# Weight halves 64 bytes past a multiple of 256, and tokens that begin at column 0, 12 or 16

## The chip, the cores and the metric

One core of a Trainium2 chip runs the kernel. The metric is the device time of one execution in microseconds. TensorE (PE in the profile) multiplies; VectorE (DVE), ScalarE (ACT) and GpSimd (POOL) work elementwise; SyncE (SP) issues most transfers. SBUF is the on-chip memory of 128 partitions, PSUM the one that TensorE writes. An address below is a byte offset within a partition of SBUF, the same in all partitions.

## The reference

Attention with a decay in place of the softmax, then a mixture of experts in two levels with one expert for each token. There are N = 4608 tokens of 512 values, and 16 experts (4 groups of 4), each with a first layer of 512 x 1024 and a second of 1024 x 512, in float32.

```python
ret = scale * (q @ k.T) * Dmat[None]          # gamma ** (i - j) for i >= j, else 0
x = (ret @ v).transpose(0, 2, 1, 3).reshape(4608, 512)
g_idx = argmax(x @ w_group); g_w = softmax at g_idx
e_idx = argmax(xg @ w_expert[g]); e_w = softmax at e_idx
h = maximum(xg[mask_e] @ w1[g, e], 0.0)
out[tok_idx] = (g_w * e_w)[:, None] * (h @ w2[g, e])
```

## The kernel before

Some 36 tiles of 128 tokens go through the attention first; each token's expert is found, and its row of x, already scaled by the product of the two weights, is scattered to its expert's region in HBM (`xs`). The expert stage follows, in 17 passes. Pass 0 takes the first 256 tokens of an expert that was picked early, while the attention still runs; passes 1 to 15 take the other experts in falling order of their counts; pass 16 takes the rest of pass 0's expert.

A pass of an expert (1 to 15) has its tokens in the columns. `xturn` turns them by VectorE into `xTf`, with 512 features as 4 chunks (`kc`) of 128 partitions. `xsplit` splits them into a rounded half `xTh` (ScalarE) and the rest `xTl` (VectorE), both of type float32r, in buffers of 4 x 384 columns. The weights come by DMA in pieces (`r`) and `wsplit` splits them in the same way into `wh0`, `wl0` (first layer) and `wh1`, `wl1` (second layer), each half 4096 bytes in a partition, three buffers for each name. `layer1` makes for each of 8 blocks of 128 hidden values (`f`) the products wh x xh, wh x xl and wl x xh over 4 chunks, 12 matmuls into one bank of PSUM. ScalarE's Relu writes `hh`, VectorE the difference `hl`, 384 columns each. `layer2` makes 12 products from them in the same manner, into 4 banks. So an expert pass has 8 x 24 = 192 matmuls. In all of them the weights are stationary (128 x 128) and the tokens move, as many columns as the pass is wide.

The width of a pass is chosen on the chip. `by_width` compares the expert's count with `LOWS[p]` and branches to matmuls that are `LOWS[p]` wide, or to those that are `CAPS[p]` wide (`CS[p]`). In pass 1 the first four blocks of layer one are always 356 wide. All writes of ScalarE and VectorE are `CS[p]` wide in either case.

Passes 0 and 16 differ: in pass 0 the first six blocks multiply plain float32 (`whole`), and in its second layer, and in both layers of pass 16, the tokens are stationary and the weights move.

The order of work is the order of the program, pinned on each engine; in a pass, block f's first layer stands before block f-1's second layer, so that at the seam of two passes one block of the new width stands before the last block of the old. Allocation goes pool by pool, in the order of the tiles in the program. In the built kernel, `wh`, `wl`, `xTh`, `xTl`, `hh` and `hl` all begin at a multiple of 256 bytes; the unused tile `lead` of 32 bytes is there ahead of them.

Of the kernel before, what the change touches and what calls it, by code (L numbers as in the profile page):

```python
# [7 lines left out]
F32 = mybir.dt.float32  # L8
F32R = mybir.dt.float32r
# [3 lines left out]
ALU = mybir.AluOpType  # L13
AX = mybir.AxisListType

P = 128
# [6 lines left out]
NKC = DM // P  # L23
NFC = F // P
CAPS = [384, 356, 342, 330, 322, 314, 310, 304, 298, 292, 288, 284, 280, 274, 266, 256]
LOWS = [0, 332, 318, 316, 316, 298, 298, 298, 292, 290, 278, 278, 268, 260, 252, 238]
CMAX = CAPS[0]
EARLY = 256
PICK = 26
WHOLE = 6  # L30
# [13 lines left out]
WQ = DQ + 4  # L44
NB = CMAX // 32
LINE = 64
# [21 lines left out]
def moe_retention(ctx, tc, qk, kv, wgt, w1, w2, c_f, out):  # L68
# [5 lines left out]
    wp = ctx.enter_context(tc.tile_pool(name="wp", bufs=1))  # L74
# [52 lines left out]
    dve, act, pool, sp = [Ordered(e_) for e_ in (nc.vector, nc.scalar, nc.gpsimd, nc.sync)]  # L127
# [29 lines left out]
    wsp = {}  # L157
    CS = [EARLY] + CAPS[1:] + [CAPS[0] - EARLY]
    NPASS = E + 1
# [10 lines left out]
    def whole(p, f):  # L170

        return p == 0 and f < WHOLE
# [6 lines left out]
    xTs = {}  # L179
# [7 lines left out]
    def ring(name):  # L187

        return gp.tile([P, NRING], F32, name=name, tag="ring", bufs=4)[:, 0 : NB * WQ]

    def nblocks(p):
        return -(-CS[p] // 32)
# [4 lines left out]
    def xpair(nm):  # L197
        return [
            gp.tile([P, NKC, CMAX], F32R, name=f"xT{x_}_{nm}", tag="xT" + x_, bufs=2) for x_ in "hl"
        ]  # L200
# [11 lines left out]
    def by_width(p, part):  # L212

        if p not in wide:
            part(CS[p])
            return
        with tc.If(wide[p] <= LOWS[p]) as narrow:
            part(LOWS[p])
        with narrow.Else():
            part(CS[p])  # L220

    def expert_of(p):
        ereg[p] = nc.values_load(
            order[0:1, p : p + 1] if p % E > 1 else eai[p % E][0:1, 0:1],
            engines=[mybir.EngineType.SP], min_val=0, max_val=E - 1,
        )

    def xload(p):
# [3 lines left out]
        if p not in ereg:  # L232
            expert_of(p)
        r0 = EARLY if p == E else 0
        nb = nblocks(p)
# [20 lines left out]
    def xpad(p):  # L256

        apart("xs", pool.indirect_dma_start(
            out=xs, out_offset=bass.IndirectOffsetOnAxis(ap={0: pad0, 1: pad1}.get(p, pads[:, p % E : p % E + 1]), axis=0),
            in_=zero, in_offset=None, bounds_check=E * NS - 1, oob_is_err=False,  # L260
        ))

    def pad(rows, e, n, cap):

        pd = sm.tile([P, 2], F32, name=f"pd_{rows.name}", tag="pd")
        dve.tensor_scalar(pd[:, 0:1], sln[:, 0:1], n, None, ALU.add)
        dve.tensor_scalar(pd[:, 1:2], pd[:, 0:1], float(cap), float(E * NS), ALU.is_ge, ALU.mult)
        dve.tensor_tensor(pd[:, 0:1], pd[:, 0:1], pd[:, 1:2], ALU.add)
        dve.scalar_tensor_tensor(rows, e, float(NS), pd[:, 0:1], ALU.mult, ALU.add)
# [4 lines left out]
    def xturn(p, part, of):  # L274

        if part == 0:
            xTs[p] = xpair(f"m{p}")
            if p == 0:

                xTf[p] = wp.tile([P, NKC, EARLY], F32, name="xTf_0", tag="wl1", bufs=3)  # L280
            else:
                xTf[p] = ring(f"xTf_{p}")[:, 0 : NKC * CMAX].rearrange("p (k c) -> p k c", k=NKC)
        nb = nblocks(p)
# [4 lines left out]
        )  # L288

    def xsplit(p, kc):  # L290
        hi, lo = xTs[p]
        C = CS[p]
        x_ = xTf[p][:, kc, :C]
        act.copy(hi[:, kc, :C], x_)
        dve.tensor_tensor(lo[:, kc, :C], x_, hi[:, kc, :C].bitcast(F32), ALU.subtract)

    def ids(p):

# [17 lines left out]
    for bp in range(B // 2):  # L316
        for j in range(9):
            if j < 8:
                b, c = 2 * bp + j // 4, j % 4
# [26 lines left out]

    sm = ctx.enter_context(tc.tile_pool(name="sm", bufs=2))
    gp = ctx.enter_context(tc.tile_pool(name="gp", bufs=1))
    ps_tr = ctx.enter_context(tc.tile_pool(name="ps_tr", bufs=1, space=PSUM))
    ps_st = ctx.enter_context(tc.tile_pool(name="ps_st", bufs=1, space=PSUM))  # L350
    ps_sm = ctx.enter_context(tc.tile_pool(name="ps_sm", bufs=2, space=PSUM))
# [189 lines left out]
    def taken():  # L541
# [5 lines left out]
        dve.tensor_reduce(c0, k2, AX.X, ALU.add)  # L547
        pad(pad0, f0, c0, EARLY)
        xpad(0)
# [13 lines left out]
    def layer1(p, f):  # L563
        i = p * NPIECE + f // 2
        C = CS[p]
        if (p, f) in ((0, 0), (0, 1)):
            ph = ps_st.tile([P, CMAX], F32, name=f"ph_{p}_{f}", tag="tr")
        elif p == 0:
            ph = psy.tile([P, CMAX], F32, name=f"ph_{p}_{f}", tag=f"py{f % 2}")
        else:  # L570
            if f % 4 not in phs:
                pool_ = (ps_sm, ps_tr, ps_sm, ps_st)[f % 4]
                phs[f % 4] = pool_.tile([P, DM], F32, name=f"ph_{f % 4}", tag="sm" if f % 2 == 0 else "tr")
            ph = phs[f % 4]
        cs = slice((f % 2) * P, (f % 2) * P + P)
        if (p, f) == (0, 0):

            hh = wp.tile([P, NKC, EARLY], F32, name="hh_0_0", tag="wl0", bufs=3)[:, 0]
        else:
            hh = mp.tile([P, CMAX], F32R, name=f"hh_{p}_{f}", tag="hh", bufs=4)  # L580
        if whole(p, f):
            for kc in range(NKC):
                pe.matmul(  # L583
                    ph[:, :C], raws[i][0][:, kc, cs], xTf[p][:, kc, :C], start=kc == 0, stop=kc == NKC - 1
                )
            hf = hh if f == 0 else hh.bitcast(F32)
            act.activation(hf[:, :C], ph[:, :C], AF.Relu)
            hts[p, f] = (hf, None)
            return
        wh, wl = wsp[i, 0]  # L590
        xh, xl = xTs[p]

        def sums(w):
            n = 0
            for kc in range(NKC):
                for a, b in ((wh, xh), (wh, xl), (wl, xh)):
                    pe.matmul(  # L597
                        ph[:, :w], a[:, kc, cs], b[:, kc, :w], start=n == 0, stop=n == 3 * NKC - 1
                    )
                    n += 1  # L600

        if (p, f) in ((1, 0), (1, 1), (1, 2), (1, 3)):
            sums(C)
        else:
            by_width(p, sums)
        C32 = 32 * nblocks(p)
        if (p, f) == (1, 0) and C32 > C:

            dve.memset(hh[:, C:C32].bitcast(F32), 0.0)
        hl = mp.tile([P, CMAX], F32R, name=f"hl_{p}_{f}", tag="hl", bufs=4)  # L610
        act.activation(hh[:, :C], ph[:, :C], AF.Relu)
        dve.scalar_tensor_tensor(
            hl[:, :C], ph[:, :C], 0.0, hh[:, :C].bitcast(F32), ALU.max, ALU.subtract
        )
        hts[p, f] = (hh, hl)
# [6 lines left out]
    with ExitStack() as ac:  # L622
# [75 lines left out]
        for t in range(LOADS - 1):  # L698
# [3 lines left out]
            if t == 3:  # L702
                sp.dma_start(wgp, wgt.rearrange("p (c e) -> p c e", c=NKC))
                sp.dma_start(cf[:, KC_ID:KC_TRI], c_f[:, KC_ID:KC_TRI])

        pw = ps_sm.tile([P, 4, P], F32, name="pw", tag="sm")
        for i in range(WARM):
            pe.matmul(pw, ones, ones.unsqueeze(1).to_broadcast([P, 4, P]), start=True, stop=True)
# [135 lines left out]
        for t in range(NT + 1):  # L844
# [63 lines left out]
            if r == 9:  # L908

                layer1(0, 0)  # L910
# [5 lines left out]
    mp = mc.enter_context(tc.tile_pool(name="mp", bufs=2))  # L916
# [15 lines left out]
    def rank_experts():  # L932
# [38 lines left out]
        el = sm.tile([P, 3], F32, name="el")  # L971
        dve.tensor_scalar(el, sln, float(EARLY), None, ALU.add)
        dve.tensor_scalar(mil, el, cr[:, 0:1], float(BIG), ALU.is_ge, ALU.mult)
# [106 lines left out]
    for p in range(E):  # L1080
        for f in range(NFC):
# [15 lines left out]
            if ahead:  # L1097
                layer2(*prev)
                for i in range(2):
                    xturn(1, i, 3)  # L1100
            layer1(p, f)
            if (p, f) == (0, 1):
                for t in range(NT - RG, NT):
# [18 lines left out]
            if (p, f) == (0, 4):  # L1122
                for kc in range(NKC):
                    xsplit(0, kc)
            if (p, f) == (0, 6):
                xturn(1, 2, 3)
                for kc in range(NKC):
                    xsplit(1, kc)
# [51 lines left out]
            if f == NFC - 2 and p:  # L1180
                for kc in range(NKC):
                    xsplit(p + 1, kc)
# [303 lines left out]
```

## Time and profile before

| | us |
|---|---|
| median of 3 runs | 577.6 (576.01 to 578.73) |
| the profiled execution | 575.34 |
| its span, first to last instruction | 573.5 |
| matmuls busy | 560.3 (98%) |
| weight loads of TensorE busy | 526.2 |
| VectorE, ScalarE, GpSimd busy | 422.7, 325.8, 260.2 |

The span is what the profile covers; the execution has 1.8 us around it. Busy times of matmuls are unions of durations that overlap, since one begins before the one ahead of it has ended: how fast they follow each other is read from their starts. The attention takes about 140 us of the span, pass 0 lies around 140 to 178, the passes 1 to 15 reach to 555, and pass 16 and the last stores end it.

### The profile page before, as it was taken

Reading aid. Unit: us, or ns where it says so; the run is one execution under the profiler, and the core shown is the slowest. Engines: PE = TensorE matmul, PEld = TensorE weight load, DVE = VectorE, ACT = ScalarE, POOL = GpSimd, SP = SyncE. Lnnn points to the kernel's source line nnn. Section 1 sums busy time; section 2 is a strip of 40 time slices with the busy share of each in tenths; the row PEclk is TensorE's granted clock in tenths of the full one; section 3 lists DMA queues with packets and bytes.
Section 4 is the critical chain, followed back from the end, with each engine's and each line's share of the span. In section 5 each row is a group of like instructions: output and inputs, shape, how many; then the busy total and the mean of one; then the engine's idle time right before and its main releaser. Section 6 shows DMA issues by size and latency. Waiting matters only on the chain.

```text
span 573.5 us, 16808 instructions
## 1 busy us (share of the span) xinstructions
PE 560.3 (98%) x6045; PEld 526.2 (92%) x6045; DVE 422.7 (74%) x985; ACT 325.8 (57%) x849; POOL 260.2 (45%) x391
## 2 busy tenths in 40 slices
PE   8998999999999999999999999999999999999995
PEld 5887788787769999999999999999999999999994
DVE  5886777878578768976767696867778677787784
ACT  5687878885346545454545454554545455455553
POOL 0022333334313037474655658374564835638554
PEclk9999999999999999999999999999999999999998
DMA  8998999956986952937375565938375585864761
GB/s 331 417 411 312 336 390 332 347 215 209 372 244 265 268 218 75 328 92 304 104 294 161 236 191 217 330 97 323 110 284 178 219 267 165 316 200 198 266 242 37
DMA packets 62409, 141.96 MB, mean 248 GB/s; under 512 B 9425, under 2 KB 30297, under 8 KB 62304
## 3 DMA queue, kind: packets, MB, share of 16 engines
q1 hardware_dynamic: 52944, 120.19, 59.5%
q0 software_dynamic: 9216, 20.28, 9.4%
q8 instruction: 72, 1.18, 0.8%
q14 instruction: 33, 0.27, 0.1%
q10 hardware_dynamic: 144, 0.05, 0.0%
HBM read 120.22 MB, written 24.81 MB: 253 GB/s over the span
## 4 chain that ended last, share of the span: by engine, by line
PE 84%; DVE 6%; DMA 4%; ACT 2%; issue 2%; SPq 1%; POOL 1%; POOLq 0%; ACTq 0%; DVEq 0%
PE ph L597 33%; PE py L1004 11%; PE py L1006 11%; PE py L1005 11%; PE px L797 4%; DMA b<-in_kv 3%; PE pxt L367 2%; PE pss L753 2%; PE px L815 2%; PE ph L583 2%; PE pst L782 2%; DVE sT L121 2%; DMA xb<-xs 1%; PE py L993 1%; PE plt L409 1%
## 5 line engine op out<-in xcount | busy, mean ns | idle before, releaser
L121 POOL DMA_INDIRECT out<-y,ii x151 | 164.8, 1091 | 61.6 <-issue 30.2
L121 DVE TENSOR_TENSOR wl<-r,wh 128x512 fp32r<-128x512 f32 x260 | 167.4, 686 | 5.3 <-ACT wh L121 2.4
L121 ACT ACTIVATE hh<-ph 128x256 fp32r<-128x256 f32 (+15 forms) x128 | 53.7, 420 | 196.1 <-PE ph L597 134.0
L121 ACT CAST wh<-r 128x512 fp32r<-128x512 f32 x260 | 147.0, 617 | 0.0
L597 PE MATMUL ph<-xTh_m,wh 128*128 128x298 f32 (+12 forms) x488 | 144.3, 296 | 0.0
L597 PE MATMUL ph<-xTl_m,wh 128*128 128x298 f32 (+12 forms) x488 | 143.8, 295 | 0.1
L597 PE MATMUL ph<-xTh_m,wl 128*128 128x298 f32 (+12 forms) x488 | 143.7, 294 | 0.0
L1004 PE MATMUL py<-hh,wh 128*128 128x298 f32 (+11 forms) x480 | 141.5, 295 | 0.0
L1006 PE MATMUL py<-hl,wh 128*128 128x298 f32 (+10 forms) x480 | 141.3, 294 | 0.0
L1005 PE MATMUL py<-hh,wl 128*128 128x298 f32 (+10 forms) x480 | 141.2, 294 | 0.0
L121 DVE SCALAR_TENSOR_TENSOR hl<-ph,hh 128x256 fp32r<-128x256 f32 (+14 forms) x122 | 56.9, 466 | 92.2 <-ACT hh L121 91.7
L597 PEld LDWEIGHTS ph<-xTl_m,wh 128*128 128x128 f32 x488 | 92.3, 189 | 0.7 <-DVE xTl_m L121 0.4
L597 PEld LDWEIGHTS ph<-xTh_m,wh 128*128 128x128 f32 x488 | 92.2, 189 | 0.7 <-ACT xTh_m L121 0.4
L597 PEld LDWEIGHTS ph<-xTh_m,wl 128*128 128x128 f32 x488 | 92.1, 189 | 0.0
L121 POOL COPY pace<-hh 1x1 f32<-1x1 f32 x140 | 34.0, 243 | 125.7 <-ACT hh L121 116.3
L1005 PEld LDWEIGHTS py<-hh,wl 128*128 128x128 f32 x480 | 90.7, 189 | 0.0
L1004 PEld LDWEIGHTS py<-hh,wh 128*128 128x128 f32 x480 | 90.7, 189 | 0.0
L1006 PEld LDWEIGHTS py<-hl,wh 128*128 128x128 f32 x480 | 90.6, 189 | 0.0
L121 POOL DMA_INDIRECT xs<-xt,sl x33 | 32.7, 992 | 103.3 <-DVE xT L121 40.1
L121 ACT ACTIVATE vs<-b,cf 128x64 f32<-128x64 f32 x288 | 72.4, 335 | 7.1 <-DMA b<-in_kv 5.9
L121 DVE TENSOR_TENSOR sT<-pss,masks 128x512 f32<-128x512 f32 x72 | 46.1, 681 | 10.4 <-PE pss L741 6.3
L797 PE MATMUL px<-sT,vs 128*64 128x128 f32 x576 | 39.4, 279 | 0.4 <-DVE xT L121 0.3
(194 smaller groups left out, 610.8 us busy)
## 6 DMA issues: line engine op xcount, KB each, us to landing
r<-in_w SPq DMA_DIRECT2D x138, 512.0 KB, 8.5
a<-in_qk SPq DMA_DIRECT2D x35, 512.0 KB
b<-in_kv SPq DMA_DIRECT2D x31, 512.0 KB, 8.1
xb<-xs SPq DMA_DIRECT2D x20, 165.0 KB, 3.7
xb<-xs SPq DMA_DIRECT2D x20, 148.5 KB, 3.0
out<-y,ii POOLq DMA_INDIRECT x151, 3.2
xb<-xs SPq DMA_DIRECT2D x12, 181.5 KB, 5.0
b<-in_kv SPq DMA_DIRECT2D x6, 256.0 KB, 6.0
```

The source lines that it names most:

```text
L121: i_ = f(*a, **k)
L367: pe.transpose(T["pxt"][:, i, :], T["xT"][:, i, :], ident)
L409: pe.matmul(plt[32 * i : 32 * i + 32], wgp[:, i, :], tiles[t]["xTg"][:, i], start=True, stop=True)
L583: pe.matmul(ph[:, :C], raws[i][0][:, kc, cs], xTf[p][:, kc, :C], start=kc == 0, stop=kc == NKC - 1)
L597: pe.matmul(ph[:, :w], a[:, kc, cs], b[:, kc, :w], start=n == 0, stop=n == 3 * NKC - 1)
L753: pe.matmul(pss[k_, o, (i + par) * P + late * D : (i + par) * P + to], T["kT"][r, i + par, k_], T["qT"][r, i + par, late * D : to], start= ...
L782: pe.matmul(pst[o * D : o * D + D, i, :], T["k"][:, h, :], T["vs"][:, h, :], start=first and i == 0, stop=True, skip_group_check=True,)
L797: pe.matmul(px[g * D : g * D + D, o, s * P : s * P + P], T["vs"][:, 4 * s + 2 * g + o, :], T["sT"][:, o, 2 * s + g, :], start=s == 0, stop ...
L815: pe.matmul(px[g * D : g * D + D, o, s * P + r * w : s * P + r * w + w], st[rows, 2 * s + g, :], T["qT"][rows, 2 * s + g, r * w : r * w + ...
L1004: pe.matmul(py[:, :w0], wh[:, f % 2, ds_], hh[:, :w0], start=st_, stop=False)
L1005: pe.matmul(py[:, :w], wl[:, f % 2, ds_], hh[:, :w], start=False, stop=False)
L1006: pe.matmul(py[:, :w], wh[:, f % 2, ds_], hl[:, :w], start=False, stop=sp_)
```

## The change

Three things change. An unused tile `lead1` of 64 bytes is allocated ahead of the split weights, so that `wh0`, `wl0`, `wh1` and `wl1` begin 64 bytes past a multiple of 256; a tile `lead2` of 192 bytes further on brings `xTh`, `xTl`, `hh` and `hl` back to a multiple of 256. Within these, each pass begins at a column of its own, `X_AT[p]` for the tokens and `H_AT[p]` for the first layer's values, the same number in both tables: 0, 12 (48 bytes) or 16 (64 bytes). And five of the narrow widths change: passes 5, 6, 7 from 298 to 302, pass 9 from 290 to 286, pass 11 from 278 to 270. The wide ones stay.

On all five engines the instructions, their order and their waits are those of before; only widths and addresses differ.

```diff
--- before.py
+++ after.py
@@ -23,8 +23,10 @@
 NKC = DM // P
 NFC = F // P
 CAPS = [384, 356, 342, 330, 322, 314, 310, 304, 298, 292, 288, 284, 280, 274, 266, 256]
-LOWS = [0, 332, 318, 316, 316, 298, 298, 298, 292, 290, 278, 278, 268, 260, 252, 238]
+LOWS = [0, 332, 318, 316, 316, 302, 302, 302, 292, 286, 278, 270, 268, 260, 252, 238]
 CMAX = CAPS[0]
+X_AT = [0, 0, 12, 12, 12, 0, 0, 0, 12, 0, 16, 0, 12, 16, 16, 16, 0]
+H_AT = [0, 0, 12, 12, 12, 0, 0, 0, 12, 0, 16, 0, 12, 16, 16, 16, 0]
 EARLY = 256
 PICK = 26
 WHOLE = 6
@@ -288,11 +290,11 @@
         )
 
     def xsplit(p, kc):
-        hi, lo = xTs[p]
-        C = CS[p]
+        x0, C = X_AT[p], CS[p]
+        hi, lo = [x_[:, kc, x0 : x0 + C] for x_ in xTs[p]]
         x_ = xTf[p][:, kc, :C]
-        act.copy(hi[:, kc, :C], x_)
-        dve.tensor_tensor(lo[:, kc, :C], x_, hi[:, kc, :C].bitcast(F32), ALU.subtract)
+        act.copy(hi, x_)
+        dve.tensor_tensor(lo, x_, hi.bitcast(F32), ALU.subtract)
 
     def ids(p):
 
@@ -346,6 +348,7 @@
 
     sm = ctx.enter_context(tc.tile_pool(name="sm", bufs=2))
     gp = ctx.enter_context(tc.tile_pool(name="gp", bufs=1))
+    gp.tile([P, 48], F32, name="lead2")
     ps_tr = ctx.enter_context(tc.tile_pool(name="ps_tr", bufs=1, space=PSUM))
     ps_st = ctx.enter_context(tc.tile_pool(name="ps_st", bufs=1, space=PSUM))
     ps_sm = ctx.enter_context(tc.tile_pool(name="ps_sm", bufs=2, space=PSUM))
@@ -577,7 +580,7 @@
 
             hh = wp.tile([P, NKC, EARLY], F32, name="hh_0_0", tag="wl0", bufs=3)[:, 0]
         else:
-            hh = mp.tile([P, CMAX], F32R, name=f"hh_{p}_{f}", tag="hh", bufs=4)
+            hh = mp.tile([P, CMAX], F32R, name=f"hh_{p}_{f}", tag="hh", bufs=4)[:, H_AT[p] :]
         if whole(p, f):
             for kc in range(NKC):
                 pe.matmul(
@@ -589,13 +592,14 @@
             return
         wh, wl = wsp[i, 0]
         xh, xl = xTs[p]
+        x0 = X_AT[p]
 
         def sums(w):
             n = 0
             for kc in range(NKC):
                 for a, b in ((wh, xh), (wh, xl), (wl, xh)):
                     pe.matmul(
-                        ph[:, :w], a[:, kc, cs], b[:, kc, :w], start=n == 0, stop=n == 3 * NKC - 1
+                        ph[:, :w], a[:, kc, cs], b[:, kc, x0 : x0 + w], start=n == 0, stop=n == 3 * NKC - 1
                     )
                     n += 1
 
@@ -607,7 +611,7 @@
         if (p, f) == (1, 0) and C32 > C:
 
             dve.memset(hh[:, C:C32].bitcast(F32), 0.0)
-        hl = mp.tile([P, CMAX], F32R, name=f"hl_{p}_{f}", tag="hl", bufs=4)
+        hl = mp.tile([P, CMAX], F32R, name=f"hl_{p}_{f}", tag="hl", bufs=4)[:, H_AT[p] :]
         act.activation(hh[:, :C], ph[:, :C], AF.Relu)
         dve.scalar_tensor_tensor(
             hl[:, :C], ph[:, :C], 0.0, hh[:, :C].bitcast(F32), ALU.max, ALU.subtract
@@ -703,6 +707,7 @@
                 sp.dma_start(wgp, wgt.rearrange("p (c e) -> p c e", c=NKC))
                 sp.dma_start(cf[:, KC_ID:KC_TRI], c_f[:, KC_ID:KC_TRI])
 
+        wp.tile([P, 16], F32, name="lead1", tag="lead", bufs=1)
         pw = ps_sm.tile([P, 4, P], F32, name="pw", tag="sm")
         for i in range(WARM):
             pe.matmul(pw, ones, ones.unsqueeze(1).to_broadcast([P, 4, P]), start=True, stop=True)
```

## Rows read from the trace of the kernel before

**Rows 1.** The page, busy time of matmuls; the granted clock in 40 slices.

```profile
PE 560.3 (98%) x6045; PEld 526.2 (92%) x6045; DVE 422.7 (74%) x985; ACT 325.8 (57%) x849; POOL 260.2 (45%) x391
...
PEclk9999999999999999999999999999999999999998
```

**Rows 2.** Windows by stage: stretch, us, busy (count) per engine, clock, DMA share, GB/s.

```profile
core 0: us, PE busy (x) PEld busy (x) DVE busy (x) ACT busy (x) POOL busy (x), PEclk, DMA share, GB/s
167.00:198.00 31.00, 30.67 (x192) 28.74 (x191) 23.57 (x52) 15.48 (x33) 4.50 (x4) 1.00 0.91 275
198.00:555.00 357.00, 357.00 (x2736) 356.81 (x2735) 266.96 (x550) 184.70 (x402) 200.86 (x293) 1.00 0.62 220
```

**Rows 3.** Waits of matmuls, 167 us to the end: all of them.

```profile
PE py L993 <- DVE hl L121: 0.2, 1, 0.2
```

**Rows 4.** Windows, matmuls alone, one width each: passes 1 to 15.

```profile
core 0: us, PE busy (x), PEclk, DMA share, GB/s
186.20:199.70 13.50, 13.50 (x92) 1.00 1.10 254
205.97:227.97 22.00, 22.00 (x152) 1.00 0.22 78
244.76:266.26 21.50, 21.50 (x152) 1.00 0.61 209
289.41:309.41 20.00, 20.00 (x152) 1.00 0.51 193
366.28:386.28 20.00, 20.00 (x152) 1.00 0.52 197
391.87:411.87 20.00, 20.00 (x152) 1.00 0.51 191
417.38:436.38 19.00, 19.00 (x152) 1.00 0.52 204
465.98:484.65 18.67, 18.67 (x152) 1.00 0.64 241
489.80:507.60 17.80, 17.80 (x152) 1.00 0.58 229
512.55:530.05 17.50, 17.50 (x152) 1.00 0.61 243
534.89:551.76 16.87, 16.87 (x152) 1.00 0.97 374
```

**Rows 5.** Windows, matmuls alone: 298 columns, pass 5's first block and second.

```profile
286.44:287.28 0.84, 0.84 (x8) 1.00 1.07 254
289.14:289.94 0.80, 0.80 (x8) 1.00 0.98 374
```

**Rows 6.** The same view: float32 matmuls of 256 columns in pass 0.

```profile
150.15:151.44 1.30, 1.30 (x7) 1.00 0.97 318
```

**Rows 7.** Groups by shape, passes 0 and 16: count, busy, mean ns, idle before.

```profile
L583 PE MATMUL ph<-xTf,r 128*128 128x256 f32 x48 | 11.6, 384 | 0.3 <-DVE xTf L121 0.3
...
L1058 PE MATMUL phn<-wh,xTh_m 128*128 128x256 f32 x16 | 4.6, 288 | 0.0
...
L993 PE MATMUL py<-wh,hhn 128*128 128x512 f32 x8 | 3.4, 425 | 0.0
```

**Rows 8.** The page's groups: Relu and difference, with their engine's idle time before.

```profile
L121 ACT ACTIVATE hh<-ph 128x256 fp32r<-128x256 f32 (+15 forms) x128 | 53.7, 420 | 196.1 <-PE ph L597 134.0
...
L121 DVE SCALAR_TENSOR_TENSOR hl<-ph,hh 128x256 fp32r<-128x256 f32 (+14 forms) x122 | 56.9, 466 | 92.2 <-ACT hh L121 91.7
```

## The prediction

> **What bounds the kernel now.** I read the page first: the matmuls are busy 98% of the span, and the granted clock is full in every slice but the last [rows 1]. So the time is that of TensorE. The windows by stage say where: from 198 to 555 us, the passes over the experts, matmuls fill 357.00 of 357.00 us, while VectorE is busy 267 and ScalarE 185, at a DMA share of 0.62 [rows 2]. The waits say the same from the other side: from 167 us to the end one matmul waited for anything, for 0.2 us [rows 3]. What shortens or lengthens a matmul in this stage moves the end by as much, and nothing else there does.
>
> Then I asked how long one matmul takes, by the distance between starts (the durations in the trace overlap, so they are of no use). I took 150 matmuls in a row of each pass, 90 in pass 1; a window counts two more, which began before it (one more in rows 6). The pace is the window's length by that number [rows 4]:
>
> 332 columns 150.0 ns; 318 146.7; 316 143.3; 298 133.3; 292 133.3; 290 133.3; 278 126.7; 268 124.4; 260 118.7; 252 116.7; 238 112.5.
>
> The reader is to see two things. First, no pace is that of the columns alone. At 2.4 GHz, the upper of the two clock levels (granted 1.00 in these rows), 298 columns are 124.2 ns; 9.2 ns are left over. The remainders are, in the same order, 11.7, 14.2, 11.7, 9.2, 11.7, 12.5, 10.8, 12.8, 10.3, 11.7 and 13.3 ns, about a tenth of the stage. Secondly, the pace is no smooth function of the columns: 290, 292 and 298 take the same 20.00 us, and the paces that repeat exactly are whole or half multiples of 6.67 ns (133.3 is 20 of them, 126.7 is 19, 146.7 is 22, 116.7 is 17.5). I call 6.67 ns a step; it is 16 columns at 2.4 GHz, and 16 columns are 64 bytes. And one width has two paces: in the first block of pass 5 six matmuls of 298 columns took 0.84 us, 140.0 ns each or 21 steps, and in its second block 0.80 us, 20 steps [rows 5]. So the remainder depends on where a matmul falls in some cycle of one step. The addresses are a plausible part of that, since the change shifts them by a step or three quarters of one against each other.
>
> **The change part by part.** Instructions, their order and what they wait for stay as they are on all five engines; no DMA changes size or queue. What changes is three widths, and addresses. All widths are even and, by routing the given inputs with the reference, the experts' counts in descending order are 330, 330, 317, 316, 315, 298, 293, 292, 289, 284, 271, 270, 267, 257, 244, 235, so each pass still takes its narrow branch (270 fits with nothing to spare).
>
> *Columns.* Each expert pass has 192 matmuls (8 blocks of F, 12 products each in both layers). Passes 5, 6, 7 get 4 columns more, pass 9 gets 4 fewer, pass 11 gets 8 fewer: 12 - 12 = 0 columns in sum. By columns alone the change is worth 0.
>
> *Addresses.* Now the stationary half and the moving columns both begin at a multiple of 256 bytes. After, the half begins at 64, and the moving columns at 0 (passes 1, 5, 6, 7, 9, 11), at 48 (passes 2, 3, 4, 8, 12) or at 64 (passes 10, 13, 14, 15). In the last group both moved by 64, so their distance is what it was; if the distance is what counts, they keep their paces, and I cost them at 0.
>
> For the others the trace of before has no row. The bounds on the remainder come from the nearest rows. Above: 140.0 ns for 298 columns, 15.8 ns [rows 5]. Below: the plain fp32 matmuls of pass 0 with 256 columns start every 216.0 ns (1.30 us for six) [rows 6]; read as two runs over the columns that is 213.3 and 2.7 ns. In between, the best settled fp32r row, 9.2 ns at 298, is the remainder of 298 against 20 whole steps, so it shows that 9.2 is enough for a matmul to keep a step, not that less is too little. The new widths ask for less: 302, 286 and 270 at column 0, and 318 at column 12, are each 7.5 ns short of a whole step (20, 19, 18, 21); 316, 268 and 332 are 8.3 short of 21, 18 and 22. I take it that in the new placement these remainders are enough and each pass settles on that whole step, as 278 to 298 do now. 7.5 lies between 2.7 and 9.2 and nearer to 9.2, so this is a choice and not a reading. Per matmul and in sum:
>
> - pass 1, 332 columns (140 matmuls; the rest has 356): 150.0 to 146.7, -0.47 us
> - pass 2: 146.7 to 140.0, 192 times, -1.28
> - passes 3 and 4: 143.3 to 140.0, 384 times, -1.28
> - passes 5 to 7: 20 steps as before, 4 columns more inside them, 0
> - pass 8, 292 columns: 19 steps would leave 5.0 ns, 20 leave 11.7; I take the middle, -0.64 (bounds 0 and -1.28)
> - pass 9: 133.3 to 126.7, -1.28
> - pass 11: 126.7 to 120.0, -1.28
> - pass 12: 124.4 to 120.0, -0.85
>
> Sum -7.1 us. Passes 0 and 16 see new addresses too: 48 fp32 matmuls in layer one, 36 fp32r ones in blocks 6 and 7, and 48 with 256 and 24 with 512 columns at the end (one product of three stands in [rows 7]). At a step each, either way, they are bounded by 1.0 us of both signs; I take 0.
>
> *Other engines.* ScalarE and VectorE write at a shifted column; ScalarE sits 196 us of the span idle before its Relu, VectorE 92 us before the difference [rows 8]. At 4 columns more for three passes (1 in 75 of about 420 and 470 ns) they stay far inside that. If the cover were gone, it would be 24 blocks by two times 6 ns, 0.3 us. A faster TensorE asks for weights 1.2% sooner at a DMA share of 0.62, which leaves room.
>
> The sum is made against the profiled execution, 575.34 us (span 573.5 and 1.8 around it): 568.2, a ratio of 0.9877. The median of the three runs is 577.6, 0.4% above it, so the forecast is 577.6 x 0.9877 = **570.5 us**.
>
> A rule speaks against all of it. The Trainium skill, "TensorE: Matmul & The Clock Gate", Part 2, step 1 (LDWEIGHTS), says that TensorE has two independent read ports into the SBUF, one for the moving operand and one for the weights, and that loading the next weights takes no bandwidth from the running matmul. By that rule, the distance between the two addresses could not matter and the sum would be 0. The trace of before agrees neither nor disagrees: 133.3 ns for three widths and two paces for one show that something waits in steps of 64 bytes, not that it is the other port. The same page, "Back-to-back issue gap", gives columns / 2.4 + 2.5 ns for a matmul; rows 4 show 9.2 to 14.2 ns.
>
> **The rivals.**
>
> *Addresses do not matter.* The steps could come from a cycle that runs on its own, with the phase alone deciding; the two paces of one width at one pair of addresses speak for it [rows 5], the rule above too. Then 298 and 302, 290 and 286 keep 20 steps and the columns cancel: **577.6**.
>
> *302 falls over the edge (slower).* 20 steps leave 9.2 ns at 298 and 7.5 at 302. If 8 is needed, passes 5 to 7 go to 21 steps, the 140.0 ns of rows 5: 6.67 ns x 576 = +3.84 us. If the placement helps nowhere else, **581.4**; if the passes with 8.3 ns still win (-0.47, -1.28, -0.85, and -0.64 in pass 8) it is +0.6, **578.2**. The point is a least remainder over 7.5 ns. For it: no settled row is under 9.2. Against it: 9.2 is only the largest width tried on that step.
>
> *More than forecast.* If the new placement takes the wait away and the remainder goes to the 2.7 ns of the fp32 rows, the eleven moved passes lose 17.7 us (302 columns to 128.5 ns, 318 to 135.2, and so on): **559.9**. One step less in passes 5 to 7 alone, on top of the forecast, gives 566.6. Against it: the 298 row is 6.5 ns above that floor.
>
> *A pass misses its narrow branch.* With a count over 270 pass 11 would run 284 columns, at 19 steps or more, and the 1.28 us are lost: 571.8. The counts above speak against it.
>
> **How the numbers follow.** The forecast, whole or in most of its passes: 0.5. More than forecast: 0.13. Addresses without effect, or gain and loss cancelling as in 578.2: 0.22. Slower, as in 581.4: 0.15. A difference under 0.5% (2.9 us) is about what a measurement of this kernel cannot tell from none; a forecast that comes half true is -3.5 us and still beyond that. So faster by over 0.5% is 0.64, within it 0.21, slower 0.15. The range goes from 563 (half way from 566.6 to 559.9) to 579 (over 578.2); it leaves out the slower rival and the deep end of the gain. The forecast's own range is 567 to 574.
>
> **What would show it.** In the profile after, 150 matmuls in a row should take 21.00 us in passes 2, 3 and 4, 20.00 in 5 to 7, 19.00 in pass 9, 18.00 in passes 11 and 12, and the old 19.00, 17.80, 17.50 and 16.87 in passes 10, 13, 14 and 15. It is wrong if passes 5 to 7 take 21.00, if the moved passes keep their paces, or if the last group changes too, which would say that the distance is not what counts. A matmul waiting for ScalarE or VectorE in the middle stage would show that my cover is gone.

## The result, and the profile after

The changed kernel takes 572.48 us (median of 18 runs), the kernel before 577.88 in runs beside it: a ratio of 0.9909, 95% interval 0.989 to 0.9929. The forecast was 570.5 us and a ratio of 0.9877. It is faster, as forecast, by three quarters of the forecast gain.

First the page of the changed kernel and its waits of matmuls from 167 us on, which answer to [rows 1, 3, 8].

```profile
PE 554.6 (97%) x6045; PEld 520.2 (91%) x6045; DVE 421.5 (74%) x985; ACT 325.9 (57%) x849; POOL 260.9 (46%) x391
...
PEclk9999999999999999999999999999999999999998
...
L123 ACT ACTIVATE hh<-ph 128x256 fp32r<-128x256 f32 (+15 forms) x128 | 53.9, 421 | 191.4 <-PE ph L601 130.5
...
L123 DVE SCALAR_TENSOR_TENSOR hl<-ph,hh 128x256 fp32r<-128x256 f32 (+14 forms) x122 | 56.6, 464 | 88.9 <-ACT hh L123 88.6
```

```profile
PE py L998 <- DVE hl L123: 0.2, 1, 0.2
```

The matmuls, as many as before, are busy 5.7 us less at the same granted clock, 4.6 us of it in the stage of the experts (below); from 167 us on one of them waits, for 0.2 us, and the idle times of ScalarE and VectorE shrink with the stage. So the gain lies in the pace of the matmuls, and nothing else took their place as the bound. The windows of the changed kernel, the view of [rows 4], 90 matmuls in pass 1 and 150 in the others (the count is two higher); widths 332, 318, 316, 302, 292, 286, 278, 270, 268, 260, 252, 238:

```profile
core 0: us, PE busy (x), PEclk, DMA share, GB/s
187.98:201.18 13.20, 13.20 (x92) 1.00 1.10 265
207.38:228.88 21.50, 21.50 (x152) 1.00 0.22 78
245.58:266.60 21.02, 21.02 (x152) 1.00 0.58 197
289.20:309.20 20.00, 20.00 (x152) 1.00 0.51 195
366.03:385.70 19.67, 19.67 (x152) 1.00 0.53 201
391.19:410.19 19.00, 19.00 (x152) 1.00 0.52 196
415.51:434.51 19.00, 19.00 (x152) 1.00 0.55 215
439.80:458.46 18.67, 18.67 (x152) 1.00 0.58 228
463.71:481.96 18.25, 18.25 (x152) 1.00 0.62 243
487.09:504.89 17.80, 17.80 (x152) 1.00 0.61 239
509.84:527.34 17.50, 17.50 (x152) 1.00 0.63 247
532.18:549.05 16.87, 16.87 (x152) 1.00 0.99 380
```

The reader is to see three groups. The last three rows, and the 19.00 of 278 columns, are the passes in which weights and tokens both moved by 64 bytes: they stand exactly as in [rows 4]. Passes 5 to 7 carry 4 columns more in the same 20.00 us. The other passes are all quicker.

How long the stage is shows in the first and last start of one product of layer two (the view of one tile's instructions; kernel before, then the changed one):

```profile
L1004 PE MATMUL py<-hh,wh x480: 273/295/354, 178.2 to 554.5; 128*128 128x298 f32 x32, 128*128 128x278 f32 x22, 128*128 128x316 f32 x21, 128*128 128x318 f32 x11
```

```profile
L1009 PE MATMUL py<-hh,wh x480: 273/292/337, 180.0 to 551.7; 128*128 128x302 f32 x32, 128*128 128x316 f32 x21, 128*128 128x318 f32 x11, 128*128 128x292 f32 x11
```

The stage is 376.3 us before and 371.7 after, 4.6 us less. The profiled spans differ by only 2.8 (573.5 and 570.7), since the attention ahead of it ended 1.8 us later in this execution. The start of the stage lies between 176.7 and 183.5 us in the fourteen profiled executions of this study. The run times scatter as much (574.4 to 580.7 us for the kernel before), which is why single spans can't be compared to a few us. The stage can, as long as its matmuls follow each other without a gap.

### The profile page after: what moved, and what is told of

It reads as the page before. It is cut to its first block, busy times and chain, and to the rows that moved or that the text cites. A ratio compares the mean times of both kernels' runs of the same rounds, so it can differ in the third digit from the quotient of the medians.

```text
span 570.7 us, 16808 instructions
## 1 busy us (share of the span) xinstructions
PE 554.6 (97%) x6045; PEld 520.2 (91%) x6045; DVE 421.5 (74%) x985; ACT 325.9 (57%) x849; POOL 260.9 (46%) x391
## 4 chain that ended last, share of the span: by engine, by line
PE 87%; DVE 5%; DMA 3%; issue 2%; ACT 1%; POOL 1%; SPq 1%; POOLq 0%; DVEq 0%
PE ph L601 33%; PE py L1011 11%; PE py L1009 11%; PE py L1010 11%; PE px L802 5%; PE pss L758 3%; PE pxt L370 3%; PE px L820 2%; PE pst L787 2%; PE ph L586 2%; PE plt L412 2%; DMA xb<-xs 1%; PE py L998 1%; DVE sT L123 1%; DMA b<-in_kv 1%
## 5 line engine op out<-in xcount | busy, mean ns | idle before, releaser
L601 PE MATMUL ph<-xTh_m,wh 128*128 128x302 f32 (+13 forms) x488 | 143.4, 294 | 0.0
L601 PE MATMUL ph<-xTl_m,wh 128*128 128x302 f32 (+13 forms) x488 | 143.0, 293 | 0.1
L601 PE MATMUL ph<-xTh_m,wl 128*128 128x302 f32 (+13 forms) x488 | 142.8, 293 | 0.0
L1009 PE MATMUL py<-hh,wh 128*128 128x302 f32 (+12 forms) x480 | 140.4, 293 | 0.0
L1010 PE MATMUL py<-hh,wl 128*128 128x302 f32 (+11 forms) x480 | 140.4, 293 | 0.0
L1011 PE MATMUL py<-hl,wh 128*128 128x302 f32 (+11 forms) x480 | 140.4, 292 | 0.0
```

The lines of the kernel that those rows point to most:

```text
L601: pe.matmul(ph[:, :w], a[:, kc, cs], b[:, kc, x0 : x0 + w], start=n == 0, stop=n == 3 * NKC - 1)
L1009: pe.matmul(py[:, :w0], wh[:, f % 2, ds_], hh[:, :w0], start=st_, stop=False)
L1010: pe.matmul(py[:, :w], wl[:, f % 2, ds_], hh[:, :w], start=False, stop=False)
L1011: pe.matmul(py[:, :w], wh[:, f % 2, ds_], hl[:, :w], start=False, stop=sp_)
```

## The experiments

The theory is that of the prediction: the distance between the first byte of the moving columns and that of the stationary half sets the pace, in stops that have to do with steps of 6.67 ns (below, a negative distance means that the tokens' offset is the smaller one). Its rivals: the widths alone do it; the moving address alone; the phase with which a pass is entered.

**Widths alone.** The kernel before with the new widths.

```diff
-LOWS = [0, 332, 318, 316, 316, 298, 298, 298, 292, 290, 278, 278, 268, 260, 252, 238]
+LOWS = [0, 332, 318, 316, 316, 302, 302, 302, 292, 286, 278, 270, 268, 260, 252, 238]
```

> The kernel before with the three new widths alone (302, 286, 270), all addresses as before. Distance theory (the start of the moving columns against the start of the stationary half sets the pace): the three widths meet the old distance 0, for which 298 was the widest seen on 20 steps. 302 columns leave their 133.3 ns, for 137 to 140; 286 stays near 133.3 and 270 near 126.7; all other passes keep the paces of before. Time +2 to +4 us, ratio 1.003 to 1.007. Width theory (the addresses do nothing, the widths do it): passes 5 to 7 at 133.3, 9 at 126.7, 11 at 124.5 as in the changed kernel, -1.7 us, ratio 0.997.

Ratio 1.0029 (0.9997 to 1.0061). Windows of passes 5, 9 and 11:

```profile
293.94:314.60 20.67, 20.67 (x152) 1.00 0.49 185
398.83:418.83 20.00, 20.00 (x152) 1.00 0.49 185
448.65:467.65 19.00, 19.00 (x152) 1.00 0.59 233
```

As expected, 302 columns take 137.8 ns, 286 and 270 stay at 133.3 and 126.7. The width theory falls: 4 columns fewer in pass 9 and 8 fewer in pass 11 are worth nothing at the old addresses, and 4 more cost 4.5 ns.

**Placement alone.** The changed kernel with the old widths.

```diff
-LOWS = [0, 332, 318, 316, 316, 302, 302, 302, 292, 286, 278, 270, 268, 260, 252, 238]
+LOWS = [0, 332, 318, 316, 316, 298, 298, 298, 292, 290, 278, 278, 268, 260, 252, 238]
```

> The changed kernel with the three old widths (298, 290, 278) and all its addresses. Distance theory, with whole steps of 6.67 ns as the stops: 298 at distance -64 stays within the 20 steps that hold 302, 133.3 ns; 290 is over the edge at 286 and takes 20 steps, 133.3 instead of 126.7; 278 in pass 11 takes 126.7 to 128.9 instead of 124.5. Time 1.7 to 2.1 us over the changed kernel, ratio to before about 0.994. Rival (the addresses alone did it, the widths are beside the point): passes 9 and 11 gain as in the changed kernel, ratio 0.991.

Ratio 1.0009 (0.9982 to 1.0036). Windows of passes 5 (298 columns) and 9 (290):

```profile
291.20:311.70 20.50, 20.50 (x152) 1.00 0.50 189
395.52:415.92 20.40, 20.40 (x152) 1.00 0.52 191
```

The widths are no side matter, so that rival falls, but the expectation's numbers were wrong too: 298 columns take 136.7 ns and 290 take 136.0, both expected at 133.3, at the distance at which 302 take 133.3. Fewer columns are slower there. In pass 12, 268 columns at column 12 take 124.5 ns here and 121.7 in the changed kernel, at the same addresses; what differs in the two kernels is the widths of passes ahead (5 to 7, 9 and 11). Neither half of the change gains anything by itself (1.0029, 1.0009); together they give 0.9909. (This run and two further down, marked there, were on another chip, on which the kernel before takes 584.6 us; the ratio is to its runs on that chip. In the profiles of these three some ten matmuls of the stage start late and cost it 1.4 to 1.6 us in all, against one matmul and 0.1 us in each of the other profiles; the windows shown are free of them.)

**Every pass at column 0, weights at 64.** The changed kernel with other columns: against the kernel before, the stationary half alone has moved (the widths are those of after).

```diff
-X_AT = [0, 0, 12, 12, 12, 0, 0, 0, 12, 0, 16, 0, 12, 16, 16, 16, 0]
-H_AT = [0, 0, 12, 12, 12, 0, 0, 0, 12, 0, 16, 0, 12, 16, 16, 16, 0]
+X_AT = [0] * 17
+H_AT = [0] * 17
```

> The changed kernel with every pass at column 0: weights 64 bytes past, distance 64 bytes in all passes. Distance theory: passes 1, 5, 6, 7, 9, 11 as in the changed kernel (146.7, 133.3, 126.7, 124.5 ns); passes 10, 13, 14, 15 leave the 126.7, 118.7, 116.7 and 112.5 ns that they had in both kernels, by 2 ns or more in at least two of them; 2, 3, 4, 8, 12 leave the paces of the changed kernel. Theory of the moving address alone (the weights' place does nothing): passes 2, 3, 4, 8, 12 return to the paces of before (146.7, 143.3, 133.3, 124.4), passes 10, 13, 14, 15 keep theirs, and the time is 2.7 us over the changed kernel, ratio 0.995.

Ratio 1.0002 (0.9967 to 1.0037). Windows of 318, 316, 302, 286, 268 and 252 columns:

```profile
206.53:228.68 22.14, 22.14 (x152) 1.00 0.21 75
245.77:267.77 22.00, 22.00 (x152) 1.00 0.61 208
291.25:311.25 20.00, 20.00 (x152) 1.00 0.47 180
393.55:412.55 19.00, 19.00 (x152) 1.00 0.48 186
466.53:485.53 19.00, 19.00 (x152) 1.00 0.64 239
513.66:530.66 17.00, 17.00 (x152) 1.00 0.62 242
```

The passes at distance -64 in both kernels (302, 286) run as in the changed one. The moving columns of 318, 316, 268 and 252 begin where they began in the kernel before, and their paces differ from it: 147.6, 146.7, 126.7 and 113.3 ns against 146.7, 143.3, 124.4 and 116.7. So the place of the weights counts, and the theory of the moving address alone falls. Of passes 10, 13, 14 and 15, two leave their paces by over 2 ns (278 columns 128.9, 252 columns 113.3), as expected, and two by 1.3 and 0.8.

**Tokens alone, weights back at 0.** The changed kernel without `lead1` and `lead2`.

```diff
-    gp.tile([P, 48], F32, name="lead2")
-        wp.tile([P, 16], F32, name="lead1", tag="lead", bufs=1)
```

> The changed kernel without its two spacer tiles: weights at a multiple of 256 again, tokens at column 0, 12 or 16. Distances: 0 in passes 1, 5, 6, 7, 9, 11; +48 bytes in 2, 3, 4, 8, 12 (it was -16); +64 in 10, 13, 14, 15 (it was 0). Distance theory: pass 1 returns to 150.0 ns, 5 to 7, 9 and 11 run as in the run with the widths alone. If the distance counts modulo 64 bytes, the other passes keep the paces of the changed kernel (143.3, 140 to 141.5, 131.1, 121.7; 126.7, 118.7, 116.7, 112.5); if it counts modulo more, they leave them. Theory of the moving address alone: every pass runs as in the changed kernel, ratio 0.991.

Ratio 1.0069 (1.0028 to 1.011), the slower side. Windows of 302 and 286 columns (distance 0) and of 278, 260, 252, 238 (distance +64):

```profile
294.46:315.46 21.00, 21.00 (x152) 1.00 0.46 174
400.56:419.89 19.33, 19.33 (x152) 1.00 0.50 188
425.28:444.28 19.00, 19.00 (x152) 1.00 0.54 211
497.44:515.44 18.00, 18.00 (x152) 1.00 0.59 229
520.41:537.61 17.20, 17.20 (x152) 1.00 0.60 236
542.39:559.13 16.75, 16.75 (x152) 1.00 0.94 355
```

Three of the last four leave their paces, so the distance does not count modulo 64 bytes. But two passes at distance 0 miss the expectation, which wanted them as in the run with the widths alone: 302 columns take 140.0 ns and not 137.8, 286 take 128.9 and not 133.3. Weights and tokens of these passes lie at the same addresses in both runs; up to there only the columns at which passes ahead begin differ (2 to 4, and 8 for the second). The likely reading is that the pass is entered otherwise and settles otherwise.

**Both at 64.** The changed kernel with weights and tokens moved together, and with the old widths (`LOWS` of the kernel before).

```diff
-X_AT = [0, 0, 12, 12, 12, 0, 0, 0, 12, 0, 16, 0, 12, 16, 16, 16, 0]
-H_AT = [0, 0, 12, 12, 12, 0, 0, 0, 12, 0, 16, 0, 12, 16, 16, 16, 0]
+X_AT = [0, 0] + [16] * 14 + [0]
+H_AT = [0, 0] + [16] * 14 + [0]
```

> The spacer tiles of the changed kernel, the old widths (298, 290, 278), and passes 2 to 15 at column 16: weights and tokens both moved by 64 bytes, distance 0 as before; pass 1 at column 0. Distance theory: passes 2 to 15 run at the paces of before in all widths (146.7, 143.3, 133.3 three times, 126.7, 124.4, 118.7, 116.7, 112.5), pass 1 at 146.7 as in the changed kernel; -0.5 us, ratio 0.999. Theory of absolute addresses: several passes leave the paces of before by 2 ns or more.

Ratio 0.9985 (0.9953 to 1.0018). Windows of 318, 316, 298, 268, 260, 252 and 238 columns:

```profile
204.01:226.01 22.00, 22.00 (x152) 1.00 0.26 95
242.81:264.31 21.50, 21.50 (x152) 1.00 0.59 197
287.47:307.47 20.00, 20.00 (x152) 1.00 0.48 181
464.04:482.71 18.66, 18.66 (x152) 1.00 0.63 241
487.85:505.65 17.80, 17.80 (x152) 1.00 0.60 235
510.61:528.11 17.50, 17.50 (x152) 1.00 0.63 245
532.95:549.82 16.87, 16.87 (x152) 1.00 1.02 384
```

They are [rows 4] again to 0.01 us in 22, and the passes not shown keep their paces too (292 and 290 columns 133.3 ns, 278 columns 126.7). So where both move by 64 bytes, the distance counts and not the addresses.

**A distance of -192.** The changed kernel with the weights at 192 and every pass at column 0 (`H_AT` as `X_AT`).

```diff
-X_AT = [0, 0, 12, 12, 12, 0, 0, 0, 12, 0, 16, 0, 12, 16, 16, 16, 0]
+X_AT = [0] * 17
-        wp.tile([P, 16], F32, name="lead1", tag="lead", bufs=1)
+        wp.tile([P, 48], F32, name="lead1", tag="lead", bufs=1)
-    gp.tile([P, 48], F32, name="lead2")
+    gp.tile([P, 16], F32, name="lead2")
```

> The changed kernel with the weights at 192 bytes past a multiple of 256 and every pass at column 0, distance -192 bytes. If the distance counts modulo 256, that is +64, and passes 10, 13, 14, 15 run as they did with the tokens 64 bytes past the weights (126.7, 120.0, 114.7, 111.6 ns). If it counts modulo 128, it is also -64: 302 at 133.3, 286 at 126.7, 270 at 124.5, 252 at 113.3. If it counts modulo 64, it is 0: 302 at 137.8 or 140, 286 at 133.3, 252 at 116.7.

One run. Windows of 260, 252 and 238 columns:

```profile
496.73:514.73 18.00, 18.00 (x152) 1.00 0.60 236
519.69:536.89 17.20, 17.20 (x152) 1.00 0.61 238
541.67:558.42 16.75, 16.75 (x152) 1.00 0.94 354
```

These are the paces of distance +64 in the run with the tokens alone, and 278 columns take 126.7 ns in both, so for these four widths the distance counts modulo 256 bytes; 302 columns take 140.0 here and 133.3 at -64, so not modulo 128.

**Column 12, 4, 8 and 24 throughout, and weights at 128.** One run each; passes 2 to 15 of the changed kernel at one column (the diff shows 12), or `lead1` and `lead2` at 32 floats each with every pass at 0. (`H_AT` as `X_AT`; column 24 and the weights at 128 ran on the other chip.)

```diff
-X_AT = [0, 0, 12, 12, 12, 0, 0, 0, 12, 0, 16, 0, 12, 16, 16, 16, 0]
+X_AT = [0, 0] + [12] * 14 + [0]
```

> The changed kernel with passes 2 to 15 at column 12, distance -16 bytes everywhere. Distance theory: passes 2, 3, 4, 8, 12, which are at column 12 in the changed kernel too, keep its paces (143.3, 140.1, 140.1, 131.1, 121.7 ns) though their neighbours move; 270 columns, at 124.5 from column 0, should come to about 122, since 268 does so from column 12. Rival (the phase at which a pass begins decides, and that comes from the pass ahead of it): at least two of the five leave those paces by 2 ns.

> The changed kernel with passes 2 to 15 at column 4 (16 bytes), distance -48 bytes. Distance theory: a third set of paces, neither that of distance -64 nor that of 0, each between columns / 2.4 + 7.5 and + 15.8 ns; pass 1 at 146.7 as before. If only the 64-byte line of the start counted, columns 0 and 4 lie in the same line and every pass runs as at column 0 (318 at 147.6, 316 at 146.7, 302 at 133.3, 286 at 126.7, 252 at 113.3 ns).

> The changed kernel with passes 2 to 15 at column 8 (32 bytes), distance -32 bytes. Distance theory: a further set of paces. If only the 64-byte line of the start counted, every pass runs as at column 0 (318 at 147.6, 316 at 146.7, 302 at 133.3, 286 at 126.7, 252 at 113.3 ns).

> The changed kernel with passes 2 to 15 at column 24, distance +32 bytes. Distance theory: a set of paces of its own; every remainder over columns / 2.4 between 7.5 and 20 ns. A pass below its pace in the changed kernel would show room for a better table: 318 under 143.3, 270 under 123.3, 252 under 113.3, 238 under 111.6 ns.

> The changed kernel with the weights 128 bytes past a multiple of 256 and every pass at column 0, distance -128 bytes. Distance theory modulo 256: a set of paces of its own, neither that of 0 nor of -64. Modulo 64 or 128: the paces of distance 0 (302 at 137.8 or 140.0, 286 at 133.3, 260 at 118.7, 252 at 116.7, 238 at 112.5 ns). It also looks for a pace lower than those known, in passes 2, 11 and 12 above all.

Windows of the run at column 12: 318, 316, 292, 302, 270 and 268 columns.

```profile
206.70:228.20 21.50, 21.50 (x152) 1.00 0.20 71
244.91:265.93 21.02, 21.02 (x152) 1.00 0.58 193
369.16:388.83 19.67, 19.67 (x152) 1.00 0.49 184
288.65:309.65 21.00, 21.00 (x152) 1.00 0.49 182
444.76:463.26 18.50, 18.50 (x152) 1.00 0.52 203
468.49:487.49 19.00, 19.00 (x152) 1.00 0.62 238
```

Four of the five passes that stand at column 12 in the changed kernel too keep its paces. The fifth, 268, takes 126.7 ns instead of 121.7: at the same distance, but behind 270 columns at -16 and not at -64. So the rival of the entry phase, which asked for two of five, does not hold as a rule, and yet it holds here, as for 302 and 286 above. By the starts of matmuls in all fourteen profiles, 28 pairs of width and distance (modulo 256) stand in more than one run: 25 settle at one pace to 0.1 ns, three do not (302 at 0: 137.8 and 140.0 ns; 286 at 0: 133.3 and 128.9; 268 at -16: 121.7, 124.5 and 126.7). Two numbers of the expectations missed: 270 columns at column 12 take 123.3 ns and not about 122, and 316 at column 4 take 150.0, a remainder of 18.3 where at most 15.8 was expected. The single times are 578.9 us at column 12, 586.3 at 4 and 580.4 at 8, beside 578.2 of the kernel before (581.9 at distance -192), and 589.3 at 24 and 586.2 with the weights at 128, beside 584.6; with the scatter of the stage's start they say only that none is quick. The paces over all distances, in ns, from windows like these:

| distance, bytes | 318 | 316 | 302 | 292 | 286 | 278 | 270 | 268 | 260 | 252 | 238 |
|---|---|---|---|---|---|---|---|---|---|---|---|
| -128 | 146.7 | 142.2 | 140.0 | 131.7 | 131.4 | 130.0 | 124.4 | 124.0 | 120.0 | 117.2 | 113.4 |
| -64 | 147.6 | 146.7 | 133.3 | 133.3 | 126.7 | 128.9 | 124.5 | 126.7 | 120.0 | 113.3 | 113.3 |
| -48 | 144.4 | 150.0 | 140.0 | 133.3 | 133.3 | 128.9 | 125.3 | 123.4 | 120.0 | 117.8 | 113.3 |
| -32 | 146.7 | 146.7 | 140.0 | 135.6 | 133.3 | 126.7 | 125.3 | 124.6 | 120.0 | 116.0 | 112.2 |
| -16 | 143.3 | 140.1 | 140.0 | 131.1 | 133.3 | 130.0 | 123.3 | 126.7 | 118.7 | 120.0 | 113.3 |
| 0 | 146.7 | 143.3 | 137.8 | 133.3 | 133.3 | 126.7 | 126.7 | 124.4 | 118.7 | 116.7 | 112.5 |
| +32 | 146.7 | 143.3 | 138.7 | 133.3 | 133.3 | 131.1 | 123.3 | 123.3 | 120.0 | 116.7 | 113.3 |
| +64 | 143.4 | 145.0 | 140.0 | 132.0 | 131.7 | 126.7 | 124.4 | 122.2 | 120.0 | 114.7 | 111.7 |
| columns / 2.4 | 132.5 | 131.7 | 125.8 | 121.7 | 119.2 | 115.8 | 112.5 | 111.7 | 108.3 | 105.0 | 99.2 |

(-128: weights at 128; +64: weights at 192; 0: the run with the widths alone.) It holds one run for each distance, so it does not show the second and third paces of 302 and 286 at 0 and of 268 at -16. The least remainder in the table is 7.5 ns, 302 and 286 at -64. Columns 0 and 4 begin in one 64-byte line and differ (302: 133.3 and 140.0), so the line of the start is not enough.

**A better table.** Three passes placed by this table (`H_AT` as `X_AT`).

```diff
-LOWS = [0, 332, 318, 316, 316, 302, 302, 302, 292, 286, 278, 270, 268, 260, 252, 238]
-X_AT = [0, 0, 12, 12, 12, 0, 0, 0, 12, 0, 16, 0, 12, 16, 16, 16, 0]
+LOWS = [0, 332, 318, 316, 316, 302, 302, 292, 292, 286, 278, 270, 268, 260, 252, 238]
+X_AT = [0, 0, 12, 12, 12, 0, 0, 12, 12, 0, 16, 0, 12, 16, 0, 32, 0]
```

> The changed kernel with three passes placed by what the other runs showed: pass 7 takes 292 columns (its count) from column 12 as pass 8 does, pass 14 begins at column 0 (distance -64, where 252 columns took 113.3 ns), pass 15 at column 32 (distance +64, where 238 took 111.6). Distance theory: pass 7 at 131.1 instead of 133.3 ns, 14 at 113.3 instead of 116.7, 15 at 111.6 instead of 112.5, all others as in the changed kernel; 192 matmuls each, -1.25 us, ratio to before 0.989. Rival (the phase with which a pass is entered decides as much as the distance): at least one of the three, or of the passes behind them, settles on another pace, and the sum is 0 or positive, ratio 0.991 or above.

571.38 us, ratio 0.9892 (0.9863 to 0.9922). Windows of passes 7, 14 and 15:

```profile
339.93:359.59 19.67, 19.67 (x152) 1.00 0.53 204
508.86:525.86 17.00, 17.00 (x152) 1.00 0.63 245
530.61:547.37 16.76, 16.76 (x152) 1.00 0.93 354
```

All three take the pace that the table gives, and the others those of the changed kernel. Here the distance theory foretold three paces from other runs. In the stage it is 1.2 us under the changed kernel (first to last start of the product shown above: 179.5 to 550.0, 370.5 against 371.7); in the run times the two intervals overlap, so that it beats the changed kernel is shown by the paces and the stage of one profile, and not by the run times.

## Why the prediction was right, step by step

*The bound.* Right: no other engine came forward, and the stage's gain is that of its matmuls. One reading was wrong and cost nothing: the 4 columns more for ScalarE and VectorE did not come, since both write `CS[p]` columns in either case.

*Distance, and the last group at 0.* Right: passes 10, 13, 14, 15 kept 19.00, 17.80, 17.50 and 16.87 us, and moving both by 64 bytes gives the paces of the kernel before in passes 2 to 15.

*The sum.* The step that was mis-sized is "each pass settles on that whole step". Forecast and measured, in us: pass 1 -0.47, -0.46; pass 2 -1.28, -0.64; passes 3 and 4 -1.28, -1.23; passes 5 to 7 0, 0; pass 8 -0.64, -0.43; pass 9 -1.28, -1.28; pass 11 -1.28, -0.42; pass 12 -0.85, -0.53. The sum is -7.1 and -5.0; the stage measures -4.6, the medians -5.4. (The -5.0 gives each pass its settled pace throughout. At the seams the matmuls are not there yet: the first and the last block of pass 12 take 126.3 and 126.7 ns a matmul, not 121.7.) Passes 0 and 16, taken at 0 within 1.0 us, are borne out for pass 16: from its first matmul's start to its last's are 11.9 us before and 11.8 after. The terms that were right are those in which a pass does stop at a whole step (22, 21, 20 and 19). Passes 2, 11 and 12 stop between: 143.3 ns is 21.5 steps, 124.5 is 18.67 and 121.7 is 18.25. A remainder of 7.5 ns was enough in passes 5 to 7 and 9, as chosen, but 318 columns at -16 and 270 at -64 did not come down to it in any run. The reason given, that a remainder large enough keeps a pass on its step, does not hold even at one distance: 298 columns at -64 have 9.2 ns to 20 steps and take 136.7, where 302 with 7.5 take 133.3. So for 302 and 286 the choice came out right by luck, and so, nearly, did the middle taken for pass 8. What the runs show in place of the rule is a stop for each pair of width and distance, often between whole steps.

*Rivals.* "Addresses do not matter" fell: the weights' place alone changes paces. "302 falls over the edge" did not happen in the changed kernel; it is what happens at every other distance of the table (137.8 to 140.0), so its price (140.0) was about right and its place was one of distance, not of the remainder. "More than forecast" did not come: no remainder under 7.5 ns was found. That the step is one of 64 bytes, as the prediction reads the 6.67 ns, no run bears out: 260, 252 and 238 columns at distance +64 do not have the paces of distance 0.

*The rule on the ports.* The Trainium skill, "TensorE: Matmul & The Clock Gate", Part 2, step 1 (LDWEIGHTS), has it that the two read ports are independent, and that loading the next weights takes nothing from the running matmul. The runs do not agree for these float32r matmuls: moving the weights alone by 64 bytes took 252 columns from 116.7 to 113.3 ns and 316 from 143.3 to 146.7. That the load of the weights and the stream of the columns delay each other in the memory would fit, but it is not shown: in the records nearly every load starts 2 to 5 ns behind a matmul whatever the pace, so that they do not tell which of the two waits, and a matmul without its own weight load was not tried. The columns / 2.4 + 2.5 ns that the prediction sets beside [rows 4] are, in the section "Back-to-back issue gap" of that page of the Trainium skill, the gap of an isolated matmul; for a stream of pairs of weight load and matmul it says that both set the spacing. So the remainders here do not speak against it.

What stays open is the rule that gives a pace from width, distance and entry phase, and with it the cause of the stops. The table is a record, not a model. The tokens and the first layer's values always moved together (`H_AT` equals `X_AT`), so the two layers were not told apart.

## What to carry to other kernels

Where matmuls follow each other without a gap, read their pace from the starts and compare it with columns / clock; a pace that is the same for several widths (133.3 ns for 290, 292 and 298 columns in [rows 4]) is a sign of stops. A few columns more can then be free and a few fewer worth nothing, or even slower, so each width has to be tried at its placement. Change width and placement together: here each alone was worth nothing and both 0.9%. A table of one width and one offset for each pass can be filled with a few runs, since one run gives a pace for every pass; the chosen table has to be run as a whole, since a pace can change with the passes ahead.

## What the hardware showed that was not expected

Fewer columns can be slower: 298 at distance -64 take 136.7 ns, 302 take 133.3. The same matmul at the same addresses keeps one of two paces for hundreds of repeats (302 columns at distance 0: 137.8 or 140.0 ns over passes 5 to 7), where two runs differ only in the passes ahead. And the paces of settled passes are simple fractions of 6.67 ns. The starts, read to the ns, show how: a few matmuls of unequal length together take a whole number of steps. For 252 columns at distance 0 gaps of 114 to 115 and 119 to 120 ns alternate, two together 35 steps; 292 at -16 repeat 129, 130, 134, three together 59; 298 at -64 repeat 136, 131, 137, 142, four together 82. The products come in threes (wh x xh, wh x xl, wl x xh), so groups of two and four do not follow the operands.
